# A planner's slot rates, the place of the output weights, and earlier splits in a fused attention and expert-lookup kernel

## The chip, the cores and the metric

The kernel runs on one core of one Trainium2 chip. The metric is device time in microseconds (us), the median of several executions of one program; lower is better.

## The reference

One layer input `x` of 2048 tokens by 512 is normalised, and two branches are added to it.

```python
xn = _layernorm(x, axis=-1)
return x + _A_ref(xn, A_wq, A_wk, A_wv, A_wo) + _B_ref(xn, B_w_q, B_k1, B_k2, B_u, B_v)
```

Branch A is attention with 32 heads of 16 columns that share one key and one value head, with an output projection `wo`. Branch B is a product-key expert lookup: for each token and each of 32 heads, scores against two sets of 64 keys, the two best of each, the two best of the four sums, a softmax over those two, and then, over all chosen experts, `gelu(x . u[expert]) * gate * v[expert]`, with 4096 rows in `u` and in `v`:

```python
act = _gelu(jnp.einsum("nd,nhkd->nhk", xf, ue))
out = jnp.einsum("nhk,nhk,nhkd->nd", g, act, ve)
```

## The kernel before

**Attention sets the beat.** The main loop (L1580 on) runs 256 pairs of key chunks, each for one unit of four heads and 512 tokens. In a pair TensorE forms the scores (`sc`, L448), ScalarE takes four exponentials of 128x1024 (`pt<-sc`, L455), and TensorE forms the weighted values (`pv`, L465). Each pair calls `att_steps` once, which calls `mid` (VectorE and GpSimd work of the expert rows) after the first two exponentials, and `fill` (score and expert matmuls) after the other two. `fill` takes as much work as a linear aim allows (about 3.6 units of planned TensorE time a pair), so every pair carries about the same TensorE work.

**Two ways for the experts.** The tokens fall into four groups of 512. For groups 0 and 1 the chosen rows of `u` and `v` are gathered: 512 slots, each an indirect DMA of 128 rows of 4 KB (`g<-in_uv_dram,idx`, L1180, issued by GpSimd) into one of `NGB = 12` row buffers; a dot with the token rows on VectorE (L1192), four small chain instructions for four slots, and an add of the weighted `v` half (`xa`, L1227), which frees the buffer. For groups 2 and 3 (`dense`, L822 on) one-hot rows are formed on VectorE (`oh`, `obs`, L971 to L974) and multiplied on TensorE (`pg`, L1004) to spread the gates over all 4096 experts, and then 32 blocks of 128 experts are done densely (`pact`, L913; `pout`, L1056). For group 2 each block's rows of `u` and `v` come raw (`rw`) into two buffers with the tag `wqt`, and are split into a high and a low f16 part (`half_split`, L865 to L882: high on ScalarE, L872; low on VectorE, L875), and the parts are also written to DRAM (`ds`); for group 3 the parts are read back, so that the raw rows' buffers are idle then.

**The order of the work.** Score items go group 0, two chunks of group 1, group 2 with its dense part, the rest of group 1, group 3 with its dense part. So there are two dense parts, each led in by some 17 pairs with one-hot rows. A number `dense_on` says where the program is, and a rate table (L1588) says how many slots are planned per pair: 2.5 while indices are being produced ahead, 2.3 for 24 pairs behind a dense part, otherwise 1.75; 0.25 beside one-hot rows (`dense_on` 2), 1.5 at the start of the dense blocks, and 2.5 in the first dense part. From pair 192 on, where the blocks run, all slots that are left are shared out evenly up to pair 252. A slot's gather may be issued when `g_next < a_next + NGB - lent[0]` (L1235): as many slots ahead of the adds as there are buffers, less the lent ones.

**Buffers that are lent.** `load_wo` (L520) brings the output weights `wo` in two tiles. With `lent[0] = 2` they lie in two of the 12 row buffers, and gathers then use 10. `lent[0]` is set at i = 124, 380 and 482 (i counts key chunks, two to a pair) and goes back to 0 when a block of four output tiles is done (L571).

**Query weights.** While group 0 runs, `wp_make` (L628) makes the next chunk's keys-times-weights tiles: four steps of `pw` (L642), then four steps with a transpose (`pwt`, L655), a high part on ScalarE (`wk`, L657) and a low part on VectorE (L658). A sum of squares (`junk`, L613) of a later chunk's weights runs on ScalarE ahead of each of the four high parts. `item` (L679) calls one step of it at k = 0 for the first two of a chunk's four items, at k = 1, and at the end. All of `psc`, `pw`, `pwt`, `pn` and `pact` take turns in three PSUM tiles of tag `x`.

Of the kernel before, what the change touches and what calls it, by code (L numbers as in the profile page):

```python
# [11 lines left out]
F32 = mybir.dt.float32  # L12
# [5 lines left out]
AF = mybir.ActivationFunctionType  # L18
OP = mybir.AluOpType
# [4 lines left out]
P = 128  # L24
S = 2048
D = 512
# [7 lines left out]
NC = 8  # L34
# [26 lines left out]
def tile_kernel(ctx, tc, x, wq, wkv, wo, wqT, kT, uv, ub, vb, out):  # L61
# [453 lines left out]
        ON[pp] = on  # L515

    DONE_A, OUTS = {}, []
    WO, lent = [], [0]

    def load_wo():  # L520
        WO.clear()
        for h in range(2):
            if lent[0]:
                assert g_next[0] - a_next[0] <= NGB - 2
                w = gtile(F32, (P, 2, D), "wo")
            else:
                if h == 0:
                    both = late[0].tile([P, 4, D], F32, name="wo", tag="wd", bufs=2)
                w = both[:, 2 * h:2 * h + 2, :]
            nc.sync.dma_start(w, wo[2 * h * P:2 * (h + 1) * P, :].rearrange("(k p) n -> p k n", p=P))  # L530
            WO.append(w)
# [83 lines left out]
    def wp_factors():  # L615
        c = factored[0]
        factored[0] += 1
        p = xtile("pn")[:, :1]
        for h in range(4):
            nc.tensor.matmul(p, ones_f, squares[:, h:h + 1], start=h == 0, stop=h == 3)  # L620
        x = small.tile([P, 1], F32, name="xw")
        nc.vector.tensor_scalar(x, p, col(K2), None, op0=OP.mult)
        factors(x.bitcast(I32), col(S_W + c), col(I_W + c))

    def wk_tile():
# [2 lines left out]
    def wp_make(c):  # L628

        wt = [big.tile([P, 2, 512], F32, name="wt", tag="da", bufs=2) for _ in range(2)]  # L630
        for h in range(4):
            for n in range(4 * c + h + 1, min(4 * c + h + 5, 4 * NC) if late[0] else 4):
                if ("raw", n // 4, n % 4) not in WC:
                    wp_load(n // 4, n % 4)
            if c == 2 and h > 1:
                wp_square()
            if c > 2 and h == 1:
                wp_factors()
            w = WC.pop(("raw", c, h))
            p = xtile("pw")  # L640
            for s in range(2):
                nc.tensor.matmul(p[s * E:(s + 1) * E, :], kTs[:, s, :], w[:, s, :], start=True, stop=True)  # L642
            nc.scalar.copy(wt[h // 2][:, h % 2, :], p)
            yield 0.9
        WC[c] = []
        if c == 2:
            yield 0.05
            wp_factors()
            yield 0.05
        for k in range(KC):  # L650
            if 1 < c < NC - 1:
                wp_square()
            p = xtile("pwt")
            for h in range(4):
                nc.tensor.transpose(p[:, h * P:(h + 1) * P], wt[h // 2][:, h % 2, k * P:(k + 1) * P], ident)  # L655
            wk = wk_tile()
            nc.scalar.activation(wk[:, 0, :], p, AF.Copy, scale=col(S_W + c))  # L657
            low = lambda p=p, wk=wk: nc.vector.scalar_tensor_tensor(wk[:, 1, :], p, col(S_W + c), wk[:, 0, :],  # L658
                                                                    op0=OP.mult, op1=OP.subtract)
            if c == 1 and late[0] is None:  # L660
                AFTER.append(low)
            else:
                low()
            WC[c].append(wk)
            (store if c > 1 else BULK.append)(lambda k=k, wk=wk: nc.sync.dma_start(d_w[c][:, k], raw(wk[:])))
            yield 0.45
# [12 lines left out]
    def item(n_, ti, make=()):  # L679
        ph, c = SEQ[n_]  # L680
        nph, nc_ = SEQ[n_ + 1] if n_ + 1 < len(SEQ) else (None, None)
        t = TPH * ph + ti
        g, j = divmod(t, GT)
        b, jb = divmod(ti, BT)
        if jb == 0:
            m8 = small.tile([P, BT, 8, 8], F32, name="m8", bufs=1)
            i8 = small.tile([P, BT, 8, 8], U32, name="i8", bufs=1)
            M8[ph, c, b], I8[ph, c, b] = m8, i8
        m8, i8 = M8[ph, c, b], I8[ph, c, b]
        p = xtile("psc")  # L690

        more = nc_ is not None and not (ph >= NSP and c == NC - 1)
        read = more and n_ + 1 >= NC
        n = 0
        for k in range(KC):
            for a, bb in TERMS:
                nc.tensor.matmul(p, XT[k][:, a, j * P:(j + 1) * P], WC[n_][k][:, bb, :],  # L697
                                 start=n == 0, stop=n == 11)
                n += 1
            if read and ti == 0 and k < 2:  # L700
                wp_read(n_ + 1, range(2 * k, 2 * k + 2))
            if k < KC - 1:
                yield 3 * UNIT
            if k == 1 or k == 0 and (n_ == 1 or ti < 2):

                yield from islice(make, 1)
        if more and nph != ph:
            load_xt(nph, j)
        for s in range(8):
            nc.vector.max(m8[:, jb, s, :], p[:, s * E:(s + 1) * E])  # L710
# [111 lines left out]
    def dense(DG, after):  # L822
# [67 lines left out]
        def later_split(b):  # L890
            def go():
                split(b)
                store(lambda: store(lambda: fetch(b + 2)))
            on_act(go)
# [72 lines left out]
        def onehot(q):  # L967
            if q < NQ:
# [5 lines left out]
                nc.vector.tensor_mul(ob, ob, bc(2, tb, NB))  # L974
                OH[q] = oa, ob

        def first_gates():

            for b in range(3):
                fetch_gates(b)  # L980
# [14 lines left out]
        for q in range(NQ):  # L995
# [30 lines left out]

            POST.append((copies, copy if ql % 2 == 0 else lambda: None))

            if q in (NQ - 16, NQ - 12):
                later_split((NQ - 16, NQ - 12).index(q))  # L1030
            if q == NQ - 3:
                on_act(lambda: halves.__setitem__(2, half_split(2, 0)))
            if q == NQ - 3:
                quiet[0] = 3
            if q == NQ - 2:
                dense_on[0] = 3
                on_act(lambda: halves.__setitem__(3, half_split(3, 0)))
                later_split(2)
            if q == NQ - 1:
                later_split(3)  # L1040
            yield 2.0
        held, ready = [], []
        stt = nc.vector.scalar_tensor_tensor
# [28 lines left out]
        for b in range(NB):  # L1072
# [67 lines left out]
            held.append((wd, vs))  # L1140
            if b > 1:
                yield 3 * UNIT
            if b == 3:
                later_split(4)
            if b == 4:
                dense_on[0] = 1
            for _ in range(b - 1 if b in (2, 3) else 0):
# [234 lines left out]
    def att_steps(d, mid, fill):  # L1382
# [48 lines left out]
            last_out_a(3)  # L1431
        if i == STEPS + 2:
            last_out_b()
        if i in (124, 380, STEPS - 30):
            lent[0] = 2
        if 128 <= i < STEPS and i % 128 == (26 if i // 128 == 2 else 10) or i == STEPS - 10:
            load_wo()
        if i == STEPS - 6:
# [134 lines left out]
    with tc.manual_schedule(engines=ENGINES):  # L1573
# [6 lines left out]
        for d in range(half + 24):  # L1580
# [4 lines left out]
            if dense_on[0] == 1:  # L1585
                pos += 2.5 if d < half * 3 // 4 else max(0.0, NSL - pos) / max(half - 3 - d, 1)
            else:
                pos += (2.5 if len(IDX) < NC * TPH else 2.3 if 0 <= d - since < 24 else 1.75, 0, 0.25, 1.5, 0.5)[dense_on[0]]  # L1588

            todo = max(min(int(pos + 0.001), g_next[0]) - d_next[0], 0) if d else 0  # L1590

# [109 lines left out]
```

## Time and profile before

| | |
|---|---|
| Time, median of 3 runs (lowest to highest) | 1825.48 us (1822.67 to 1826.49) |
| Profiled execution: its own time, its span | 1830.28 us, 1828.5 us |
| Busy share of the span | PE 93%, DVE 87%, ACT 73%, POOL 37% |
| Slots (gathers, dots, adds) | 512 each |
| Exponentials `pt<-sc` | 1024, four to a pair |

PE is TensorE, DVE VectorE, ACT ScalarE, POOL GpSimd; SP issues most transfers. In a row of a group, behind the bar, stand the busy time, the mean ns of one, and the idle time of the engine just before such instructions with what ended it.

### The profile page before, as it was taken

To read this page: it belongs to the slowest core of one execution; us is meant where nothing else is said; L and a number is where in the kernel's file an instruction comes from. 1 tells how busy PE (TensorE), PEld (TensorE's weight loads), DVE (VectorE), ACT (ScalarE), POOL (GpSimd) and SP (SyncE) were. 2 spreads that over 40 slices of the span, in tenths; PEclk is the share of its full clock that TensorE was granted. 3 is DMA by queue.
4 is the path that set the end of the run, shared out by engine and by line. 5 is a ranking of instruction groups with operands and counts; after the bars stand their busy time and mean duration, and the time that the engine had idled before them with its cause. 6 is when DMAs were issued, how large, how long until landed. Compare 5 with 4: busy or idle time off the path is not lost.

```text
span 1828.5 us, 35039 instructions
## 1 busy us (share of the span) xinstructions
PE 1708.1 (93%) x11070; PEld 602.5 (33%) x11070; DVE 1592.1 (87%) x6345; ACT 1328.2 (73%) x1785; POOL 684.6 (37%) x923
## 2 busy tenths in 40 slices
PE   7989998999998898999999999999988987899998
PEld 3433332333333332333333333333333322333332
DVE  7748888999998976899998899999989666998995
ACT  6468777867767987888887666666678865677774
POOL 1024444435552102344343455445520124444550
PEclk9999999999999999999999999999999998999999
DMA  7378778998763569999998967966444757999994
GB/s 263 120 255 318 272 241 280 315 325 320 264 218 114 188 218 279 297 336 316 323 336 313 328 237 255 289 201 213 131 147 166 247 183 246 322 315 342 311 300 159
DMA packets 257272, 470.97 MB, mean 258 GB/s; under 512 B 107316, under 2 KB 118596, under 8 KB 257084
## 3 DMA queue, kind: packets, MB, share of 16 engines
q0 software_dynamic: 73728, 268.47, 43.5%
q1 hardware_dynamic: 182940, 199.59, 33.9%
q8 instruction: 87, 1.43, 0.3%
q14 instruction: 101, 0.83, 0.1%
q10 hardware_dynamic: 416, 0.66, 0.1%
HBM read 407.36 MB, written 56.39 MB: 254 GB/s over the span
## 4 chain that ended last, share of the span: by engine, by line
PE 38%; DVE 34%; ACT 7%; DMA 7%; issue 4%; POOL 2%; SPq 0%; another core or an unknown queue 0%; ACTq 0%; DVEq 0%; POOLq 0%
PE pv L465 12%; DVE i L712 7%; PE sc L448 7%; DVE xa L1227 7%; PE pact L913 5%; PE pout L1056 5%; DVE g L1192 5%; DVE m L710 5%; PE psc L697 5%; DMA g<-in_uv_dram,idx 5%; ACT pt L455 4%; DVE oh L971 2%; PE pwo L563 1%; PE pw L642 1%; POOL g L1180 1%
## 5 line engine op out<-in xcount | busy, mean ns | idle before, releaser
L455 ACT ACTIVATE pt<-sc 128x1024 f32<-128x1024 f32 x1024 | 989.1, 1026 | 309.6 <-PE sc L448 254.4
L1180 POOL DMA_INDIRECT g<-in_uv_dram,idx x512 | 541.3, 1057 | 911.7 <-DVE xa L1227 408.6
L465 PE MATMUL pv<-pt,vaug 128*32 128x512 f32 x4096 | 504.3, 611 | 0.0
L448 PE MATMUL sc<-qa,kaug 64*128 64x512 f16 x2048 | 326.8, 385 | 57.9 <-ACT pt L455 50.8
L1227 DVE SCALAR_TENSOR_TENSOR xa<-g,w,xa 128x512 f32<-128x512 f32 x512 | 372.8, 745 | 0.0
L1192 DVE CUSTOM_DVE_ANT_0 g<-g,xa 128x512 f32<-128x512 f32 x512 | 335.0, 682 | 42.6 <-DMA g<-in_uv_dram,idx 41.9
L697 PE MATMUL psc<-wk,xt 128*128 128x512 f16 x1536 | 357.6, 381 | 10.4 <-DVE wk L658 7.5
L448 PEld LDWEIGHTS <-kaug 64*128 64x128 f16 x2048 | 83.6, 94 | 402.2 <-issue 396.9
L697 PEld LDWEIGHTS <-xt 128*128 128x128 f16 x1536 | 141.0, 98 | 208.3 <-issue 59.5
L712 DVE FIND_INDEX8 i<-m,psc 128x8 uint32<-128x64 f32 x1024 | 206.5, 222 | 0.3 <-issue 0.3
L465 PEld LDWEIGHTS pv<-pt,vaug 128*32 128x32 f32 x4096 | 108.3, 110 | 256.9 <-issue 256.9
L913 PE MATMUL pact<-xt,wk 128*128 128x512 f16 x768 | 183.3, 384 | 5.4 <-DVE wk L875 3.9
L1056 PE MATMUL pout<-wk,wd 128*128 128x512 f16 x768 | 176.1, 380 | 1.7 <-DVE gates L1105 1.4
L710 DVE MAX8 m<-psc 128x8 f32<-128x64 f32 x1024 | 146.0, 214 | 10.1 <-PE psc L697 8.8
L913 PEld LDWEIGHTS <-wk 128*128 128x128 f16 x768 | 69.4, 99 | 106.8 <-issue 30.9
L1056 PEld LDWEIGHTS <-wd 128*128 128x128 f16 x768 | 73.2, 98 | 94.9 <-issue 11.0
L971 DVE TENSOR_TENSOR oh<-io,tr 128x2048 f16<-128x2048 f16 x64 | 78.0, 1218 | 9.4 <-ACT tr L939 5.5
L712 DVE MATCH_VALUE_LOAD i<-m,psc 128x8 f32 x1024 | 72.1, 70 | 0.0
L756 POOL CAST fi<-i 128x64 f32<-128x64 uint32 x32 | 8.3, 258 | 148.2 <-DVE i L712 144.5
L1129 DVE SCALAR_TENSOR_TENSOR gy<-gy,pact 128x512 f32<-128x512 f32 x60 | 40.8, 680 | 22.4 <-ACT gy L1128 17.7
L1059 DVE SCALAR_TENSOR_TENSOR da<-pout,cols,da 128x512 f32<-128x512 f32 x72 | 52.9, 744 | 6.1 <-PE pout L1056 4.5
L1208 ACT ACTIVATE gth<-gy 128x4 f32<-128x4 f32 x128 | 26.9, 210 | 41.9 <-DVE gy L1202 33.6
(218 smaller groups left out, 1481.5 us busy)
## 6 DMA issues: line engine op xcount, KB each, us to landing
wk<-dw SPq DMA_DIRECT2D x96, 256.0 KB
wqt<-in_wqT_dram SPq DMA_DIRECT2D x32, 512.0 KB
un<-in_uv_dram SPq DMA_DIRECT2D x16, 1024.0 KB
ds<-wk SPq DMA_DIRECT2D x64, 256.0 KB
gates<-dg SPq DMA_DIRECT2D x64, 256.0 KB
wk<-ds SPq DMA_DIRECT2D x64, 256.0 KB
dg<-gst SPq DMA_DIRECT2D x14, 928.0 KB
dw<-wk SPq DMA_DIRECT2D x32, 256.0 KB
```

The lines of the kernel that those rows point to most:

```text
L448: nc.tensor.matmul(p[:, b, :], kaug[o:o + 64, kc * P:(kc + 1) * P], QA[u][o:o + 64, i, :], start=True, stop=True)
L455: nc.scalar.activation(PT[u, kc, i], p, AF.Exp, scale=SCALE)
L465: nc.tensor.matmul(PV[u][32 * j:32 * j + 32, :], vaug[:, kc, :], pt[:, b, :], start=kc == 0, stop=kc == 15)
L697: nc.tensor.matmul(p, XT[k][:, a, j * P:(j + 1) * P], WC[n_][k][:, bb, :], start=n == 0, stop=n == 11)
L710: nc.vector.max(m8[:, jb, s, :], p[:, s * E:(s + 1) * E])
L712: nc.vector.max_index(i8[:, jb, s, :], m8[:, jb, s, :], p[:, s * E:(s + 1) * E])
L913: nc.tensor.matmul(p, us[:, a, k * P:(k + 1) * P], XT[k][:, c, :], start=n == 0, stop=n == 11)
L971: nc.vector.tensor_tensor(out=oa, in0=num(P), in1=bc(0, tb, P), op=OP.is_equal)
L1056: nc.tensor.matmul(p, wd[0][:, a, j * P:(j + 1) * P], vs[:, c, :], start=n == 0, stop=n == last)
L1180: nc.gpsimd.indirect_dma_start(out=gt, out_offset=None, in_=uv, in_offset=bass.IndirectOffsetOnAxis(ap=IDX[ph, c, ti][:, s:s + 1], axis=0))
L1192: nc.vector.tensor_tensor_reduce(u, u, XN[TPH * ph + ti], scale=1.0, scalar=0.0, op0=OP.mult, op1=OP.add, accum_out=a[:, i:i + 1])
L1227: nc.vector.scalar_tensor_tensor(acc, v, w[:, i:i + 1], acc, op0=OP.mult, op1=OP.add)
```

## The change

The change has five parts:

- The slot rate beside one-hot rows is 0.5 a pair in place of 0.25, and the rate 2.3 behind a dense part holds for 32 pairs in place of 24.
- From i = 380 on no row buffer is lent: `wo` lies in the two raw rows' buffers (tag `wqt`). The first loan, at i = 124, stays.
- In the one-hot stage the splits of blocks 0 to 4 stand at other steps q (of 32). Before: blocks 0 and 1 at 16 and 20, block 2's first half at 29, its rest and block 3's first half at 30, block 3's rest at 31, block 4 in the dense blocks (at b = 3). Now: 14, 17, then 20 and 22 for block 2, 24 and 26 for block 3, 28 and 30 for block 4.
- The four squares that stand beside a chunk's transposes come 0, 2, 1, 1 in place of 1, 1, 1, 1, and only chunk 1's items call a step of `wp_make` at k = 0.
- The factor of a chunk's scale (`xw`, one column) is taken by ScalarE in place of VectorE.

```diff
+            elif ON_ROWS[0]:
+                w = big.tile([P, 2, D], F32, name="wo", tag="wqt", bufs=2)
...
-        nc.vector.tensor_scalar(x, p, col(K2), None, op0=OP.mult)
+        nc.scalar.activation(x, p, AF.Copy, scale=col(K2))
...
-            if 1 < c < NC - 1:
+            for _ in range((0, 2, 1, 1)[k] if 1 < c < NC - 1 else 0):
                 wp_square()
...
-            if k == 1 or k == 0 and (n_ == 1 or ti < 2):
+            if k == 1 or k == 0 and n_ == 1:
...
+        half = lambda b: on_act(lambda: halves.__setitem__(b, half_split(b, 0)))
+        SPLITS = {NQ - 18: lambda: later_split(0), NQ - 15: lambda: later_split(1),
+                  NQ - 12: lambda: half(2), NQ - 10: lambda: later_split(2),
+                  NQ - 8: lambda: half(3), NQ - 6: lambda: later_split(3),
+                  NQ - 4: lambda: half(4), NQ - 2: lambda: later_split(4)}
...
-            if b == 3:
-                later_split(4)
...
-        if i in (124, 380, STEPS - 30):
+        if i == 124:
             lent[0] = 2
+        if i == 380:
+            ON_ROWS[0] = 1
...
-                pos += (2.5 if len(IDX) < NC * TPH else 2.3 if 0 <= d - since < 24 else 1.75, 0, 0.25, 1.5, 0.5)[dense_on[0]]
+                pos += (2.5 if len(IDX) < NC * TPH else 2.3 if 0 <= d - since < 32 else 1.75, 0, 0.5, 1.5, 0.5)[dense_on[0]]
```

VectorE's queue in the first one-hot stage, from the 22nd one-hot step on, before. `oh` and `obs` are one-hot rows, `gst` the copy of spread gates, `ISA g,act` a slot's dot and `ISA act` the read of its sum.

```order
L974 TENSOR_TENSOR obs<-obs,tr 128x512
L1192 ISA g,act<-g,xa 128x512
L1192 ISA act 128x1
L971 TENSOR_TENSOR oh<-io,tr 128x2048
L973 TENSOR_TENSOR obs<-io,tr 128x512
L974 TENSOR_TENSOR obs<-obs,tr 128x512
L1009 COPY gst<-pg 128x32x16
L971 TENSOR_TENSOR oh<-io,tr 128x2048
L973 TENSOR_TENSOR obs<-io,tr 128x512
L974 TENSOR_TENSOR obs<-obs,tr 128x512
L971 TENSOR_TENSOR oh<-io,tr 128x2048
```

Here one dot stands in a stretch of several one-hot steps. The same place now; `gq`, `gy` and `ga` are the chain of four slots, `wk<-rw` the low part of a split.

```order
L976 TENSOR_TENSOR obs<-obs,tr 128x512
L877 SCALAR_TENSOR_TENSOR wk<-rw,cols,wk 128x512
L1192 ISA g,act<-g,xa 128x512
L1192 ISA act 128x1
L1201 SCALAR_TENSOR_TENSOR gq<-act 128x4
L1202 SCALAR_TENSOR_TENSOR gy<-gq,act 128x4
L1203 TENSOR_TENSOR ga<-act,gg 128x4
L973 TENSOR_TENSOR oh<-io,tr 128x2048
L975 TENSOR_TENSOR obs<-io,tr 128x512
L976 TENSOR_TENSOR obs<-obs,tr 128x512
L1017 COPY gst<-pg 128x32x16
```

Between the same one-hot rows VectorE now has a split's low part and, at this point, the chain of the second four slots of the stage: in the stage stand 8 dots and 8 adds where 4 and 4 stood.

ScalarE's queue while a chunk's weights are made, before: `pt` are exponentials, `junk` squares, `wk` high parts.

```order
L455 ACTIVATE pt<-sc 128x1024 x2
L613 ACTIVATE junk,squares<-wqt 128x1024
L657 ACTIVATE wk<-pwt,cols 128x512
L613 ACTIVATE junk,squares<-wqt 128x1024
L657 ACTIVATE wk<-pwt,cols 128x512
L455 ACTIVATE pt<-sc 128x1024 x2
```

And for a chunk now:

```order
L455 ACTIVATE pt<-sc 128x1024 x2
L659 ACTIVATE wk<-pwt,cols 128x512
L615 ACTIVATE junk,squares<-wqt 128x1024 x2
L659 ACTIVATE wk<-pwt,cols 128x512
L455 ACTIVATE pt<-sc 128x1024 x4
```

The first high part now stands ahead of the squares, the second behind two of them; the sums over a chunk are the same.

More of the change, by code (lines that the diff above doesn't have):

```diff
@@ L517, in tile_kernel @@
     DONE_A, OUTS = {}, []
-    WO, lent = [], [0]
+    WO, lent, ON_ROWS = [], [0], [0]
     def load_wo():
@@ L1027, in dense @@
             POST.append((copies, copy if ql % 2 == 0 else lambda: None))
[L1029 to L1032, printed above, removed]
+            if q in SPLITS:
+                SPLITS[q]()
             if q == NQ - 3:
@@ L1036, in dense @@
                 dense_on[0] = 3
[L1037 to L1040, printed above, removed]
             yield 2.0
```

## The prediction

> **What bounds the kernel now.** I read the page first (busy shares, costliest groups), then the busy times by stage, the exponentials by stage (they count the pairs), the groups of single stages, and the timeline where TensorE stood still.
>
> ```profile
> span 1828.5 us, 35039 instructions
> PE 1708.1 (93%) x11070; PEld 602.5 (33%) x11070; DVE 1592.1 (87%) x6345; ACT 1328.2 (73%) x1785; POOL 684.6 (37%) x923
> L1227 DVE SCALAR_TENSOR_TENSOR xa<-g,w,xa 128x512 f32<-128x512 f32 x512 | 372.8, 745 | 0.0
> L1192 DVE CUSTOM_DVE_ANT_0 g<-g,xa 128x512 f32<-128x512 f32 x512 | 335.0, 682 | 42.6 <-DMA g<-in_uv_dram,idx 41.9
> ```
>
> TensorE and VectorE are both near full, so the question is where one of them waits. VectorE waits for gathered rows in all 42 us. The groups of two dense parts, first and last, say where:
>
> ```profile
> L1192 DVE CUSTOM_DVE_ANT_0 g<-g,xa 128x512 f32<-128x512 f32 x110 | 71.4, 682 | 0.0
> ...
> L1192 DVE CUSTOM_DVE_ANT_0 g<-g,xa 128x512 f32<-128x512 f32 x141 | 92.3, 684 | 42.6 <-DMA g<-in_uv_dram,idx 41.9 <-issue 0.5
> ```
>
> The first row is 723.8 to 1024.1 us (44 pairs, 2.5 slots a pair, 12 row buffers): no wait at all. The second is 1464 to 1795.5 (46 pairs, 141 slots, 3.07 a pair, 10 buffers in the first 8 pairs and the last 11): all of the 42 us. What it costs in time is read from the exponentials, four to a pair:
>
> ```profile
> core 0: us, ACT busy (x), PEclk, DMA share, GB/s
> 1464.00:1693.10 229.10, 115.21 (x121) 0.96 0.87 282
> 1693.10:1795.50 102.40, 62.04 (x64) 1.00 0.91 299
> 723.80:1024.10 300.30, 169.31 (x178) 0.99 0.96 317
> 1173.10:1327.40 154.30, 92.92 (x96) 1.00 0.61 199
> ```
>
> The last 16 pairs take 102.4 / 16 = 6.40 us each, and 24 pairs of score items at 1173 take 6.43: this is the beat when TensorE alone binds, since the planner gives each pair the same TensorE work. The 30 pairs from 1464 to 1693.1 take 7.64. At 6.45 they would take 193.5, so some 35 us are lost there.
>
> ```profile
> 1676.92 0.69 DVE L1192 CUSTOM_DVE_ANT_0 g<-g,xa 128x512 f32<-128x512 f32 x1 [1.93 <-DMA g<-in_uv_dram,idx]
> 1681.66 0.72 ACT L1130 ACTIVATE gy<-gy,cols 128x512 f32<-128x512 f32 x1 [1.22 <-DVE gy L1129]
> 1676.30 1.92 PE L465 MATMUL pv<-pt,vaug 128*32 128x512 f32 x16
> 1683.35 0.39 PE L448 MATMUL sc<-qa,kaug 64*128 64x512 f16 x2 [3.18 <-ACT pt L455]
> 1684.80 3.30 PE L465 MATMUL pv<-pt,vaug 128*32 128x512 f32 x16
> ```
>
> This is one such loss: a dot waits 1.93 us for its rows, the dense block's `gy` behind it on VectorE is late, the tanh and the exponentials behind it on ScalarE too, and TensorE stands for 3.18 us; then 16 matmuls that took 1.92 us take 3.30.
>
> ```profile
> 1464.00:1492.40 28.40, 28.04 (x172) 9.75 (x170) 19.35 (x50) 21.03 (x30) 6.38 (x6) 1.00 0.55 169
> 1492.40:1536.00 43.60, 30.02 (x150) 9.62 (x151) 26.52 (x65) 19.58 (x27) 14.01 (x13) 0.86 0.73 225
> 1536.00:1693.10 157.10, 145.88 (x866) 48.00 (x865) 139.18 (x350) 111.58 (x151) 76.31 (x71) 0.97 0.97 318
> ```
>
> (After the length stand PE, PEld, DVE, ACT and POOL busy, the granted clock, DMA share and rate.) Idle time alone is 229.1 - 203.9 = 25 us; the other 10 are slow matmuls, at a granted clock of 0.86 and 0.97. [...]
>
> **The change part by part.**
>
> *Last dense part, -28 us.* By the rate table 17 pairs beside one-hot rows carry 0.25 more, twice (4.25 each), and 8 pairs 2.3 in place of 1.75 (4.4): 12.9 slots are done earlier, which leaves 46 x 3.07 - 12.9 = 128 slots for the 46 pairs, 2.79 a pair, with 12 buffers throughout. The first dense part waited for nothing at 2.5 and 12 buffers, at a DMA share of 0.96. This one lies between: 12 buffers last 4.3 pairs, against 4.8 there and 3.3 (10 buffers) to 3.9 (12) before. At 3.9, in the 22 pairs from 1536 on, 157.1 - 22 x 6.45 = 15 us were lost, part of it while the queue caught up. DMA demand falls by 12.9 x 128 x 4 KB = 6.8 MB. I keep 7 of the 35 us as still lost, half of those 15 (bounds 2 and 17).
>
> *First one-hot stage, +7.*
>
> ```profile
> core 0: us, PE busy (x) PEld busy (x) DVE busy (x) ACT busy (x) POOL busy (x), PEclk, DMA share, GB/s
> 577.30:658.60 81.30, 69.71 (x902) 29.94 (x891) 78.52 (x133) 75.48 (x93) 6.12 (x4) 1.00 0.48 159
> 658.60:702.90 44.30, 44.07 (x258) 14.82 (x261) 27.00 (x63) 35.72 (x47) 10.29 (x10) 1.00 0.83 268
> 1173.10:1327.40 154.30, 152.92 (x947) 51.49 (x945) 151.92 (x1002) 97.15 (x118) 80.00 (x156) 1.00 0.61 199
> 1345.30:1426.90 81.60, 70.06 (x902) 29.65 (x899) 77.70 (x131) 74.54 (x90) 2.15 (x2) 1.00 0.42 141
> ...
> L875 DVE SCALAR_TENSOR_TENSOR wk<-rw,cols,wk 128x512 f16<-128x512 f32 x3 | 2.2, 744 | 0.0
> ```
>
> VectorE binds this stage (78.5 of 81.3). A slot costs it (335.0 + 372.8) / 512 = 1.38 us, 1.4 with its share of the chain. Four more slots (8 for 4 in the order) are 5.6 us. Of the splits' low parts 3 stood here, some 6 will: 3 x 0.74 = 2.2. One us goes into the 2.8 idle. ScalarE takes 3 more high parts, under its 5.8 idle. What the splits leave, 658.6 to 702.9, is full on TensorE (44.1 of 44.3), so nothing is won there.
>
> *Second one-hot stage, +4.6:* four slots, 5.6, less one us of the 3.9 idle; no splits are formed there.
>
> *Pairs 158 to 165, +4:* 4.4 slots are 6.2 us on a VectorE that has 2.4 us to spare in 154.3 (last but one row). The rest stays as lag and is paid at the one-hot rows' lead-in, which waits for the last item's gates. Bounds 0 and 6.
>
> *Weights of the first phase, -1.*
>
> ```profile
> 205.00:281.00 76.00, 70.73 (x426) 23.68 (x418) 66.41 (x342) 57.06 (x84) 32.11 (x42) 0.96 0.77 256
> 281.00:301.00 20.00, 15.31 (x95) 5.89 (x96) 13.80 (x71) 15.05 (x24) 5.35 (x5) 0.91 0.77 248
> 288.03 0.75 DVE L658 SCALAR_TENSOR_TENSOR wk<-pwt,cols,wk 128x512 f16<-128x512 f32 x1 [4.98 <-ACT wk L657]
> 288.84 2.72 PE L697 MATMUL psc<-wk,xt 128*128 128x512 f16 x6 [2.69 <-DVE wk L658]
> ```
>
> Here TensorE stands 10 us in 96, where a high part sits behind squares on ScalarE and an `x` tile is not freed. With two steps of `wp_make` an item, not three, three, two and none, two waits a chunk for the item just finished go, but each item now takes the tile of the one before it, one step later. One high part a chunk comes ahead of the squares, another behind two. I cannot sign this; -8 to +6. The factor's move takes one column from one queue to another, beside exponentials: 0.
>
> *Placing `wo` in idle buffers, 0:* the two transfers stay; only their place changes.
>
> Sum: -28 + 6.8 + 4.6 + 4 - 1 = -13.6, call it -14. The profiled execution took 1830.3 us (1.8 beside its span) and becomes 1816. It lies 0.26% over the median 1825.5, which goes to **1811.5**.
>
> **Rivals.**
>
> *Gathers wait all the same.* From 1536 to 1693.1 the DMA share was 0.97 at 318 GB/s; if the transfers themselves set the wait, two more buffers only lengthen the queue. Then half of the 28 comes, 14, against 14.4 paid: 1825. Against it: 0.96 at 317 GB/s without a wait in the first dense part.
>
> *VectorE becomes the bound (slower).* Its place is the one-hot stages and pairs 158 to 165: nothing of 7.8 + 5.6 + 6.2 = 19.6 us is absorbed. It decides when the last part gives back less than that, as by idle time alone, 25, less 10 still lost: +5, 1830.
>
> *A stall goes that I leave in place.*
>
> ```profile
> 704.85 2.56 ACT L872 ACTIVATE wk<-rw,cols 128x512 f16<-128x512 f32 x4
> 709.32 0.75 DVE L875 SCALAR_TENSOR_TENSOR wk<-rw,cols,wk 128x512 f16<-128x512 f32 x1
> 710.12 4.45 PE L913 MATMUL pact<-xt,wk 128*128 128x512 f16 x10 [3.88 <-DVE wk L875]
> ```
>
> Block 5 waits for its split; with its slow matmuls some 6 us. The earlier splits stop at block 4, and the four high parts of blocks 5 and 6 stand in ScalarE's queue as before, so I expect it again. If it goes, and the first phase gives 6: -25, 1800.
>
> *GpSimd and VectorE hinder each other.*
>
> ```profile
> L1180 POOL DMA_INDIRECT g<-in_uv_dram,idx x4 | 6.1, 1530 | 53.6 <-DVE xa L1227 53.0 <-issue 0.6
> ```
>
> A gather's issue beside one-hot rows took 1.53 us. If VectorE stood still that long, eight more in the two stages would cost 12: -2, 1823.5. [...] The row shows GpSimd slowed, not VectorE.
>
> **How the numbers follow.** 0.2% is 3.65 us, about what a measurement of this kernel can tell from no change. My forecast has 0.60: its bounds added as squares (up 10, 7, 2 and 1; down 5, 7 and 4) make it -23 to -1, 0.57 faster and 0.03 same. The stall goes: 0.10, faster. Gathers still wait: 0.13, mostly same (0.09), 0.03 faster, 0.01 slower. Hindrance: 0.05, same. VectorE binds: 0.12, slower 0.11, same 0.01. Faster 0.70, same 0.18, slower 0.12. The range 1798 to 1824 takes in the forecast's own range, the stall's case and most of the waiting case; the slower case and an edge of the others stay outside.
>
> **What would show it.** Right: dots in the last dense part wait under 10 us for gathers, and its 30 first pairs take 6.5 to 6.7 us each; both one-hot stages are 4 to 8 us longer with VectorE full; the wait before 710 is there again. Wrong: 20 us or more of waits for gathers at the new rate, a one-hot stage longer by over 12 us, or a first phase (124 to 355) that moves by over 8 us either way.

## The result, and the profile after

The changed kernel takes 1812.81 us (median of 5 runs, 1808.76 to 1815.56), the kernel before 1826.49 us beside it (5 runs, 1822.67 to 1828.03): a ratio of 0.9925, 95% interval 0.9908 to 0.9942, or some 13.7 us. The profiled execution took 1814.29 us with a span of 1812.6, 15.9 us less than the span of before. The forecast was 1811.5. The sum came out, but several of its terms did not come about as they were argued, and that is what most of the experiments are on.

The rows of the page of the changed kernel that answer to the first ones of before:

```profile
span 1812.6 us, 35046 instructions
PE 1705.5 (94%) x11070; PEld 601.1 (33%) x11070; DVE 1592.4 (88%) x6337; ACT 1328.8 (73%) x1793; POOL 685.1 (38%) x923
L1227 DVE SCALAR_TENSOR_TENSOR xa<-g,w,xa 128x512 f32<-128x512 f32 x512 | 372.2, 745 | 0.0
L1192 DVE CUSTOM_DVE_ANT_0 g<-g,xa 128x512 f32<-128x512 f32 x512 | 334.3, 682 | 2.6 <-DMA g<-in_uv_dram,idx 2.6
```

The engines do the same work, but the dots' waits for gathered rows fell from 42.6 to 2.6 us. The busy times by stage, first one-hot stage, pairs 158 to 181, second one-hot stage, and then the last dense part in three pieces (us, then PE, PEld, DVE, ACT and POOL busy, granted clock, DMA share, rate):

```profile
572.20:662.90 90.70, 73.65 (x898) 30.07 (x891) 87.54 (x155) 77.47 (x98) 7.55 (x6) 0.94 0.50 171
1176.80:1332.20 155.40, 149.04 (x908) 49.52 (x906) 153.19 (x985) 93.34 (x115) 82.44 (x160) 0.99 0.64 213
1356.30:1444.60 88.30, 74.44 (x904) 30.36 (x896) 83.07 (x147) 74.83 (x92) 10.49 (x8) 0.94 0.55 178
1481.30:1535.30 54.00, 53.89 (x320) 18.38 (x316) 48.02 (x117) 40.57 (x56) 20.99 (x20) 1.00 0.83 263
1535.30:1676.90 141.60, 140.20 (x866) 47.09 (x864) 127.35 (x315) 110.14 (x148) 66.46 (x62) 1.00 0.96 314
1676.90:1779.30 102.40, 102.13 (x632) 34.46 (x630) 93.59 (x234) 78.23 (x104) 41.88 (x39) 1.00 0.86 289
```

In the last dense part TensorE is now full throughout, at a granted clock of 1.00: 30 pairs take 54.0 + 141.6 = 195.6 us, 6.52 each, where they took 229.1. The stages above it became longer. Counted by the exponentials (pair d begins with exponential 4d), the time went like this, in us; columns 4 to 6 are kernels of the experiments below:

| Pairs | before | after | `wo` alone | rates alone | `wo` and first phase |
|---|---|---|---|---|---|
| 5 to 60 (weights of the first phase) | 386.2 | 381.4 | 385.4 | 382.8 | 378.5 |
| 65 to 82 (first one-hot stage) | 81.3 | 90.7 | 81.3 | 88.3 | 81.2 |
| 89 to 91 (block 5's stall) | 20.8 | 21.3 | 21.4 | 20.8 | 20.9 |
| 135 to 158 | 149.0 | 148.0 | 148.5 | 148.0 | 148.4 |
| 158 to 181 | 148.1 | 155.4 | 148.2 | 154.7 | 148.4 |
| 184 to 201 (second one-hot stage) | 81.6 | 88.3 | 83.2 | 86.0 | 81.6 |
| 207 to 215 (last dense part) | 72.0 | 54.0 | 54.1 | 54.0 | 54.0 |
| 215 to 237 | 157.1 | 141.6 | 150.7 | 141.2 | 148.3 |
| 237 to 253 | 102.5 | 102.4 | 102.5 | 102.4 | 102.5 |

The last dense part gives 33.6, the first phase with what lies ahead of pair 65 5.1 (pair 65 begins at 572.2, before at 577.3); the one-hot stages take 9.4 and 6.7, pairs 135 to 181 6.3. That is -33.6 - 5.1 + 9.4 + 6.7 + 6.3 = -16.3, against -15.9 in the spans. One-hot stages at the same slot rate differ by up to 3 us between kernels, and the granted clock goes with it. At the old rate the second one took 81.6 to 81.9 us at a clock of 1.00, 83.2 at 0.98 and 84.8 at 0.96; at the new rate 85.5 to 86.0 at 0.98, and 88.2 and 88.3 at 0.94. The two kernels compared here stand at opposite ends, 1.00 before and 0.94 after, so some 2 us of the 6.7 go with the clock of this execution.

The groups of the first one-hot stage on VectorE, before and after:

```profile
L971 DVE TENSOR_TENSOR oh<-io,tr 128x2048 f16<-128x2048 f16 x31 | 37.7, 1218 | 1.5 <-PE pg L1004 1.5
L1192 DVE CUSTOM_DVE_ANT_0 g<-g,xa 128x512 f32<-128x512 f32 x5 | 3.4, 673 | 0.0
L1227 DVE SCALAR_TENSOR_TENSOR xa<-g,w,xa 128x512 f32<-128x512 f32 x4 | 2.8, 744 | 0.0
```

```profile
L973 DVE TENSOR_TENSOR oh<-io,tr 128x2048 f16<-128x2048 f16 x31 | 37.8, 1218 | 1.1 <-PE pg L1012 1.0
L1192 DVE CUSTOM_DVE_ANT_0 g<-g,xa 128x512 f32<-128x512 f32 x10 | 6.7, 679 | 0.0
L1227 DVE SCALAR_TENSOR_TENSOR xa<-g,w,xa 128x512 f32<-128x512 f32 x8 | 5.7, 745 | 0.0
L877 DVE SCALAR_TENSOR_TENSOR wk<-rw,cols,wk 128x512 f16<-128x512 f32 x7 | 5.2, 746 | 0.0
```

Five dots, four adds and four low parts more (7, where 3 stood) are 3.3 + 2.9 + 3.0 = 9.2 us, and VectorE's busy time rose by 87.5 - 78.5 = 9.0 in a stage that became 9.4 longer: the added instructions were paid in full. This is a long execution of the stage, though: with 11 and with 10 row buffers (below), at the same rate and with the same splits, it took 88.7 and 88.5 us at a granted clock of 0.98, with 8 dots and 8 adds, and VectorE idle for 2.7 and 2.4 us. The one-hot operation itself takes 1218 ns as before. Block 5's stall stands where it stood:

```profile
709.05 2.56 ACT L874 ACTIVATE wk<-rw,cols 128x512 f16<-128x512 f32 x4
713.52 0.75 DVE L877 SCALAR_TENSOR_TENSOR wk<-rw,cols,wk 128x512 f16<-128x512 f32 x1
714.33 4.45 PE L915 MATMUL pact<-xt,wk 128*128 128x512 f16 x10 [3.88 <-DVE wk L877]
```

### The profile page after: what moved, and what is told of

Read it like the earlier page. It is cut to its first block, busy times and chain, and to the rows that moved or that the text cites. A ratio compares the mean times of both kernels' runs of the same rounds, so it can differ in the third digit from the quotient of the medians.

```text
span 1812.6 us, 35046 instructions
## 1 busy us (share of the span) xinstructions
PE 1705.5 (94%) x11070; PEld 601.1 (33%) x11070; DVE 1592.4 (88%) x6337; ACT 1328.8 (73%) x1793; POOL 685.1 (38%) x923
## 4 chain that ended last, share of the span: by engine, by line
PE 58%; DVE 20%; ACT 8%; issue 3%; DMA 3%; POOL 1%; SPq 0%; ACTq 0%; DVEq 0%; another core or an unknown queue 0%; POOLq 0%
PE pv L465 17%; PE sc L448 10%; PE psc L699 10%; PE pout L1058 8%; PE pact L915 7%; ACT pt L455 5%; DVE i L714 4%; DVE xa L1227 3%; DVE m L712 3%; DVE g L1192 3%; PE pwo L565 2%; DVE oh L973 2%; PE pw L644 1%; ACT wk L874 1%; DMA rsb<-dinv 1%
## 5 line engine op out<-in xcount | busy, mean ns | idle before, releaser
L1227 DVE SCALAR_TENSOR_TENSOR xa<-g,w,xa 128x512 f32<-128x512 f32 x512 | 372.2, 745 | 0.0
L973 DVE TENSOR_TENSOR oh<-io,tr 128x2048 f16<-128x2048 f16 x64 | 77.9, 1218 | 10.0 <-PE pg L1012 4.7
L1110 DVE SCALAR_TENSOR_TENSOR gy<-gy,gates 128x512 f32<-128x512 f32 x60 | 41.4, 690 | 22.1 <-ACT gy L1132 17.3
```

The lines of the kernel that those rows point to most:

```text
L973: nc.vector.tensor_tensor(out=oa, in0=num(P), in1=bc(0, tb, P), op=OP.is_equal)
L1227: nc.vector.scalar_tensor_tensor(acc, v, w[:, i:i + 1], acc, op0=OP.mult, op1=OP.add)
```

## The experiments

**The parts one by one.** The first four kernels each have one part of the change on the kernel before (1825.44 us beside them, 1821.87 to 1831.22). The theory (A in each) is the prediction's: waits for gathers in the last dense part come from too few slots of look-ahead, and every other part acts where it stands.

*The place of `wo` alone.*

```diff
+            elif ON_ROWS[0]:
+                w = big.tile([P, 2, D], F32, name="wo", tag="wqt", bufs=2)
...
-        if i in (124, 380, STEPS - 30):
+        if i == 124:
             lent[0] = 2
+        if i == 380:
+            ON_ROWS[0] = 1
```

> The kernel before with the output weights placed in the raw rows' buffers alone; rates, splits and first phase as before. Theory A (how many row buffers lie ahead decides the wait for gathers): the first 8 pairs of the last dense part, which had 10 buffers, go from 72 to about 54 us; the 22 pairs behind them, at 12 buffers and 3.07 slots a pair, keep some 5 of the 15 us they lost; the one-hot stages and pairs 158 to 180 are unchanged. The whole is 25 us faster, 1800. Theory B (the slot rate, and with it the transfers' own rate, decides): the last part stays within 6 us of before, 1820 to 1826.

Measured: 1805.82 us (1802.62 to 1806.52), ratio 0.9875 (0.9854 to 0.9896). The dots of its trace:

```profile
L1194 DVE CUSTOM_DVE_ANT_0 g<-g,xa 128x512 f32<-128x512 f32 x512 | 333.9, 680 | 21.3 <-DMA g<-in_uv_dram,idx 21.3
```

Half of the waits are gone, 24.3 us of the last part's loss come back, and next to nothing is paid for it. Theory A holds for the first 8 pairs (54.1 us); the 22 behind them keep more than its 5 us (150.7, where the changed kernel takes 141.6). This one part is faster than the whole change.

*The rates alone*, 0.5 beside one-hot rows and 32 pairs at 2.3, with buffers lent as before.

```diff
-                pos += (2.5 if len(IDX) < NC * TPH else 2.3 if 0 <= d - since < 24 else 1.75, 0, 0.25, 1.5, 0.5)[dense_on[0]]
+                pos += (2.5 if len(IDX) < NC * TPH else 2.3 if 0 <= d - since < 32 else 1.75, 0, 0.5, 1.5, 0.5)[dense_on[0]]
```

> The kernel before with the two slot rates alone (0.5 beside one-hot rows, 2.3 held for 32 pairs); two row buffers stay lent. Theory A: one-hot stages +6.7 each, pairs 158 to 180 +7; the last part at 2.79 slots and 10 buffers (3.6 pairs of rows ahead) gets back some 15 of 35 us; the whole 5 us slower, 1831. Theory B: the last part gets back 30 or more, the whole 10 us faster, 1816.

Measured: 1811.41 us (1807.62 to 1811.87), ratio 0.9913 (0.9894 to 0.9932). Theory A, by which the rates do little without the buffers, falls. The last part gets back all 34 us, with 9.9 us of waits left, and the stages ahead pay 7.0, 6.6 and 4.4. So rates and place do not add: either removes the pile-up of pairs 207 to 215, and with the rates there is nothing left for the place to win there.

*The earlier splits alone.*

```diff
+            if q in SPLITS:
+                SPLITS[q]()
...
-            if b == 3:
-                later_split(4)
```

> The kernel before with the earlier splits alone. Theory A: VectorE binds the first one-hot stage, so the low parts that move into it cost 2 to 3 us there, and nothing comes back, since TensorE was full behind it and block 5's split waits as before: 1829. Rival: the splits relieve the start of the dense blocks, and the stage 658 to 724 us gets 3 to 6 us shorter: 1823.

Measured: 1827.12 us (1821.62 to 1834.69, 10 runs), ratio 1.0005 (0.9987 to 1.0022): no difference to be told. The first one-hot stage took 83.1 for 81.3, the stall 20.8 as before.

*The first phase's edits alone*: squares, steps of an item, and the factor.

```diff
-            if 1 < c < NC - 1:
+            for _ in range((0, 2, 1, 1)[k] if 1 < c < NC - 1 else 0):
...
-            if k == 1 or k == 0 and (n_ == 1 or ti < 2):
+            if k == 1 or k == 0 and n_ == 1:
```

> The kernel before with the three edits to the first phase alone (two steps of weight making an item, squares 0, 2, 1, 1, the factor on ScalarE). Theory A: pairs 5 to 31 get 4 us shorter as in the changed kernel, all else stays: 1822. Rival: those 4 us are chance of one execution, and the time is that of before, 1826.

Measured: 1824.28 us (1816.83 to 1828.15, 10 runs), ratio 0.9988 (0.9971 to 1.0004). The interval holds both no change and 5 us; pairs 5 to 60 took 380.3 us in the trace, against 386.2.

**Taking parts together.** Three kernels beside one another, and one on look-ahead (the kernel before beside them: 1826.9 us, 1824.73 to 1829.55).

*The change without the earlier splits* (the lines of `SPLITS` left as they were before).

> The changed kernel with the old places of the splits of blocks 0 to 4; everything else as changed. Theory A (every part acts only in the stretch where its instructions stand, and the earlier splits only add three low parts of 0.74 us to a full VectorE in the first one-hot stage): that stage, 90.7 us with all parts, goes to 88 (as with the rates alone, 88.3), the rest stays, 1810 us against 1812.8. Theory B (the earlier splits relieve the dense blocks that follow, so that they pay together with the rates): pairs 82 to 91, 65.8 us, get longer by 3 or more, 1815.

Measured: 1808.63 us (1807.19 to 1811.13), ratio 0.99 (0.9882 to 0.9918). The first one-hot stage took 88.1, the pairs behind it 65.1 as ever. Theory A. The splits' part is 2.6 us here, but at clocks of 0.94 and 0.98; alone it is 1.8 us at 1.00, where the six kernels without splits and at the old rate agree within 0.1 us.

*The same without the new rates*: the place of `wo` and the first phase's edits alone.

```diff
-2.3 if 0 <= d - since < 32 else 1.75, 0, 0.5, 1.5, 0.5)
+2.3 if 0 <= d - since < 24 else 1.75, 0, 0.25, 1.5, 0.5)
```

> The kernel before with the place of wo and the first phase's edits (squares, steps, factor); rates and splits stay old. Theory A (the gains of the two stretches add): 1805.8 with the place alone, less 1.2 to 3, so 1803 to 1804.6, and the last dense part as with the place alone (54 for pairs 207 to 215, 151 for 215 to 237). Theory B (the first phase's gain is only the spread of executions): 1806, no difference from the place alone.

Measured: 1795.3 us (1793.82 to 1802.03), ratio 0.9836 (0.9809 to 0.9862). 8 us better than theory A, most of it because pairs 5 to 60 took 378.5 us, 6.9 less than with the place alone. Beside the last kernel, on the same chip, the new rates cost 1808.63 - 1795.3 = 13.3 us (11.7 by the two ratios). The trace says how: they save 148.3 - 141.2 = 7.1 in pairs 215 to 237, and take 6.9 in the first one-hot stage, 6.2 in pairs 158 to 181 and 6.6 in the second one-hot stage (at a clock of 0.94 for 1.00), together 19.7.

*The slots moved to where VectorE has room.* In the pairs behind each one-hot stage VectorE was busy for 27.0 of 44.3 us and less.

```diff
-1.75, 0, 0.25, 1.5, 0.5)
+1.75, 0, 0.25, 2.25, 0.5)
...
-                    sums = min(sums, 2)
+                    sums = min(sums, 3 if dense_on[0] == 3 and d > 80 else 2)
```

> As the one with the place of wo and the first phase's edits, and the slots that the change takes beside one-hot rows are taken instead in the 7 and 6 pairs behind them, where VectorE was busy for 27 of 44 and 21 of 37 us: the rate there is 2.25 in place of 1.5, and up to 3 adds a pair in place of 2. Theory A (a slot costs time only where VectorE is full): 13 x 0.75, some 9.75 slots leave the last dense part, whose pairs 215 to 237 go from 151 to 144 or less, the 13 pairs take 1 us more at most, both one-hot stages stay at 81 to 83: 1797. Theory B (those pairs carry the first blocks' chains on VectorE, and more dots ahead of them hold TensorE up, or leave no rows ahead for the dense part): those pairs or the ones behind them get 7 us longer, 1804 or more.

Measured: 1796.5 us (1791.72 to 1801.92), ratio 0.9823 (0.9796 to 0.985), no better than the kernel without it. Both theories hold in part: pairs 215 to 237 took 141.1 (148.3), but pairs 89 to 91 grew from 20.9 to 23.7 and pairs 91 to 158 by 3.9, behind the first one-hot stage; the wait of block 5's matmuls itself is 3.95 us for 3.88, and what the rest comes from was not followed. Behind the second one-hot stage nothing got longer.

*Four buffers lent in place of two, with the new rates.*

```diff
-            lent[0] = 2
+            lent[0] = 4 if i == 380 else 2
```

> The kernel before with the new rates alone, and with 4 row buffers lent in place of 2 from i = 380 until the output block is done, so that gathers use 8 there. Theory A (a dot waits when its gather is issued less than some 8 us ahead of it, and that lead is set by the slots between gather and add over the slots a pair, so a lower rate and more buffers stand for each other): at 2.8 slots a pair 8 buffers give a lead as short as 10 did at 3.07, dots wait again 15 us or more in pairs 207 to 215, which go from 54 back to 65 to 80, and the time from 1811.4 to 1820 to 1835. Theory B (what counts is the demand on the transfers that the rate sets, not the buffers): waits stay near 10 us, 1812.

Measured: 1806.2 us (1803.38 to 1809.27), ratio 0.989 (0.9871 to 0.9909), and pairs 207 to 215 took 54.0. This reads as theory B, but the trace shows that the test was none. By the program's count the gathers of slots 380 and 381 come in pair 203, which began at 1446 us. GpSimd in that stretch, with four lent, and with two:

```profile
start us, us, engine line op out<-in xcount [idle before <-releaser]
1409.40 1.15 POOL L1180 DMA_INDIRECT g<-in_uv_dram,idx  x1 [33.01 <-DVE xa L1227]
1413.20 1.88 POOL L1180 DMA_INDIRECT g<-in_uv_dram,idx  x1 [2.66 <-DVE rc L503]
```

```profile
1412.44 1.20 POOL L1180 DMA_INDIRECT g<-in_uv_dram,idx  x1 [30.86 <-DVE xa L1227]
1413.94 0.96 POOL L1180 DMA_INDIRECT g<-in_uv_dram,idx  x1 [0.30 <-issue]
```

The two gathers go at the same place in both. The program's count only sets where a gather stands in the code; GpSimd has its instructions in the same order in both kernels and ran ahead (with four lent, 33 us before pair 203 began); what held the first of the two gathers was an add (33.01 and 30.86 us of idle, `<-DVE xa L1227`), which frees a buffer, and not the count. While the program lends four, slots 380 to 407 go out with nine others between gather and add (one with eight), ten buffers in all, as with two lent from slot 382 on; the count would allow eight. So the look-ahead here was the ten buffers that were really free for it. The kernel is in effect another run of the rates alone.

**The buffers themselves.** So the next two kernels have fewer of them: the changed kernel with 10, and with 11 (beside the kernel before, 1827.68 and 1826.06 us).

```diff
-NGB = 12
+NGB = 10
```

> The changed kernel with 10 row buffers in place of 12 in the whole run (with 4 less that the program lends, gathers were issued as early as with 2 less, since a gather is held on the chip by its buffer and not by the program's count; here the buffers themselves are fewer). Theory A (look-ahead and rate stand for each other: at 2.8 slots a pair ten buffers are 3.6 pairs, between the 3.3 that cascaded into waits and the 3.9 that lost 9 of 157): dots wait 15 to 30 us in the last dense part, half of it is lost, 1820 to 1828. Theory B (the rate alone decides, ten are enough at 2.8 as in pairs 207 to 215 with the rates alone): waits at most 10 us, 1813 to 1816. The first dense part at 2.5 a pair, 4 pairs ahead, stays at 300 us in both.

Measured: 1875.27 us (1870.36 to 1882.09), ratio 1.0282 (1.0235 to 1.0329). Theory A, and far beyond it: two buffers are worth 62 us. In the profiled executions the difference is 57 us, and not all of it lies in the last dense part: pairs 215 to 237 take 28.0 more and pairs 237 to 253 9.6, but pair 65 also begins 11.1 us later, pairs 91 to 135 take 4.6 more, and 253 to 255 6.2. Dots wait 13.3 us for gathers ahead of pair 65 and 8.7 in the first dense part, where they waited for nothing with 12 buffers and where the expectation saw no loss. What makes pairs 253 to 255 longer was not followed. The dots of pairs 215 to 237, and the busy times of that stretch:

```profile
L1192 DVE CUSTOM_DVE_ANT_0 g<-g,xa 128x512 f32<-128x512 f32 x61 | 40.9, 684 | 40.3 <-DMA g<-in_uv_dram,idx 40.1
```

```profile
1494.30:1548.30 54.00, 53.89 (x320) 18.38 (x316) 44.45 (x109) 40.67 (x56) 18.75 (x18) 1.00 0.83 259
1548.30:1717.90 169.60, 147.26 (x866) 48.21 (x864) 129.26 (x322) 111.20 (x149) 66.98 (x62) 0.96 0.85 267
1717.90:1829.90 112.00, 104.52 (x632) 34.97 (x630) 89.98 (x224) 78.50 (x103) 45.98 (x43) 0.98 0.79 257
```

The first eight pairs take no longer than with 12 buffers; there a dot's gather was issued 9.0 us ahead (median), behind them 7.5. The transfers are less busy than with 12 buffers (0.85 against 0.96): it is not their rate that is short. And with 11:

> The changed kernel with 11 row buffers in the whole run. With 12 its dots in pairs 215 to 237 were issued 11.1 us ahead (median) and waited 2.6 us in all, with 10 it was 7.5 us and 40.3 us. Theory A (the lead falls smoothly with the buffers, some 1.8 us a buffer, and waits grow fast below 9 us, as in the kernel before, 8.7 us and 18.2 us): lead 9 to 9.5 us, 8 to 18 us of waits in those pairs, which take 146 to 154 us, and 1818 to 1835 us in all. Theory B (adds free the buffers in fours, so that 11 buffers hold no more than 10, and only a third group of four makes the difference): lead 7.5 to 8 us, 35 us or more of waits, 1865 to 1875.

Measured: 1814.45 us (1809.35 to 1815.65), ratio 0.993 (0.9911 to 0.995). The waits are theory A's, the lead, 8.8 us, a little under it; the total lies 4 us below its range, since these waits cost 4.4 us and those of pairs 237 to 253, 9.3 us, nothing (102.4 us as with 12):

```profile
L1192 DVE CUSTOM_DVE_ANT_0 g<-g,xa 128x512 f32<-128x512 f32 x61 | 40.3, 682 | 14.0 <-DMA g<-in_uv_dram,idx 13.7
```

Here are all kernels in pairs 215 to 237. The lead is the time from a gather's issue on GpSimd to its dot on VectorE, both in slot order, and its median is given; a dot counts where it begins.

| Kernel | Buffers | Dots there | Lead, us | Waits, us | Length, us |
|---|---|---|---|---|---|
| 10 buffers, new rates | 10 | 61 | 7.5 | 40.3 | 169.6 |
| earlier splits alone | 12 | 69 | 8.6 | 17.8 | 156.3 |
| before | 12 | 69 | 8.7 | 18.2 | 157.1 |
| `wo` and first phase | 12 | 68 | 8.7 | 11.9 | 148.3 |
| `wo` and squares (below) | 12 | 68 | 8.7 | 11.7 | 149.3 |
| first phase alone | 12 | 69 | 8.8 | 20.9 | 160.4 |
| 11 buffers, new rates | 11 | 60 | 8.8 | 14.0 | 146.0 |
| `wo` alone | 12 | 68 | 8.9 | 15.1 | 150.7 |
| best (below) | 12 | 65 | 9.1 | 5.3 | 141.3 |
| rates alone | 12 | 61 | 10.0 | 2.9 | 141.2 |
| slots moved | 12 | 61 | 10.3 | 0.8 | 141.1 |
| four lent, new rates | 12 | 61 | 10.5 | 3.8 | 141.2 |
| without the splits | 12 | 59 | 10.8 | 1.8 | 141.2 |
| after | 12 | 59 | 11.1 | 2.6 | 141.6 |

Lead goes up with buffers and down with slots a pair. From 10 us on the waits are under 4 us, at 7.5 they are 40; close to 9 us the median does not order the kernels (11.7 to 20.9 us of waits at leads of 8.6 to 8.9). In the eight traces that have landings for this stretch, the median from a gather's issue to its landing is 6.5 to 7.5 us, so that a median lead of 7.5 us leaves next to nothing over. The lead goes the same way in pairs 207 to 215, where either part removes the pile-up: it was 8.4 us there before, with 22.2 us of waits, 9.2 with the rates alone (6.8 us of waits), 9.6 with the place alone (2.5) and 15.2 with both (none). Some 5 us of waits in 22 pairs cost nothing (the best version: 5.3 us of waits, and 141.3 us long).

**The first phase.** The place of `wo` with the squares 0, 2, 1, 1 alone:

```diff
-            if 1 < c < NC - 1:
+            for _ in range((0, 2, 1, 1)[k] if 1 < c < NC - 1 else 0):
```

> The kernel before with the place of wo (1805.8) and the squares 0, 2, 1, 1; steps of an item as before. Theory A (the gain of the first phase, pairs 5 to 60 from 385 to 380, comes from the first high part of a chunk, which no longer stands behind a square): pairs 5 to 60 take 379 to 382, 1800 to 1802. Theory B (it comes from two steps an item in place of three): 384 to 387, 1804 to 1807.

Measured: 1801.62 us (1798.45 to 1806.23), ratio 0.9877 (0.984 to 0.9915). Pairs 5 to 60 took 379.7 us: theory A. Before, and with the squares moved:

```profile
152.10:538.30 386.20, 369.19 (x2266) 126.22 (x2261) 361.19 (x2107) 294.18 (x415) 181.75 (x287) 0.98 0.85 286
```

```profile
148.70:528.40 379.70, 364.26 (x2254) 125.68 (x2246) 360.81 (x2107) 294.65 (x414) 181.51 (x287) 1.00 0.86 290
```

Of the 6.5 us only 1.6 are idle time of TensorE (17.0 to 15.4); the other 4.9 are its busy time, at a granted clock of 1.00 for 0.98. In the traces of the kernels before and after, the clock falls to half 14 and 13 times for 3.41 or 6.83 us, and once for less at the end of each. The first such stretch in the kernel before, with the wait ahead of it:

```profile
218.87 0.63 PE L655 MATMUL pwt<-ident,wt 128*128 128x128 f32 x4 [2.65 <-DVE i L712]
219.90:223.30 3.40, 3.40 (x18) 0.73 (x20) 3.04 (x8) 2.26 (x3) 0.14 (x1) 0.50 0.89 308
```

Pairs 5 to 60 have four of them before (from 219.9, 237.0, 288.2 and 376.9 us) and one with the squares moved (from 230.3). Three stretches fewer, at half the clock, are 3 x 3.41 / 2 = 5.1 us, which accounts for the 4.9. The longest single waits ahead of these five were 2.65, 1.10, 2.69, 2.06 and 1.10 us. The number of stretches is partly chance: the five kernels with the old squares have two to four and take 382.9 to 386.9 us, the seven with the new ones and 12 buffers (all but this one with the item's steps and the factor too) one or two and 378.5 to 381.4. With half the time of its stretches taken off, the five are at 379.3 to 380.3 and the seven at 376.3 to 378.7, so some 2 us come by the waits and the rest by how often the clock fell. The ratio alone does not tell this kernel from the one with `wo` alone (0.9875).

**The best version.** From `wo` and the first phase: the higher rate behind the second one-hot stage alone, the earlier splits, and block 5's split asked for a block sooner, which the earlier split of block 4 allows.

```diff
-1.75, 0, 0.25, 1.5, 0.5)
+1.75, 0, 0.25, 2.25 if d > 128 else 1.5, 0.5)
...
-                    sums = min(sums, 2)
+                    sums = min(sums, 3 if dense_on[0] == 3 and d > 128 else 2)
...
+                        if b == 2 and DG == NSP:
+                            later_split(5)
+                        elif b == 3 and DG > NSP:
+                            later_split(5)
...
-            if b % 2 and b > 1:
+            if b % 2 and b > 3:
                 later_split(b + 2)
```

> The kernel with the place of wo and the first phase's edits (1795.3), and three things more: the rate 2.25 and up to 3 adds behind the second one-hot stage alone; the earlier splits; and block 5's split asked for in block 2 in place of block 3. Theory A (each acts in its stretch): pairs 215 to 237 from 148 to 142; pairs 89 to 91 from 20.9 to 13 to 15, since block 5's low part no longer stands in VectorE's queue behind a block's gy; pairs 65 to 82 from 81.2 to 83 for the splits' low parts; 1785 to 1788. Theory B (block 5 waits for its raw rows, which the first blocks' transfers hold up, and the stall only moves): pairs 89 to 93 keep their length, and the splits' cost remains, 1791 to 1794.

Measured: 1787.96 us (1783.16 to 1790.66), ratio 0.9799 (0.9764 to 0.9834), the fastest of all kernels here, 37 (by the ratio) to 40 us (by the medians) below the kernel before. Theory A holds in each of its figures. The stall is gone, and with it its slow matmuls; the first matmuls of the two blocks in pairs 89 to 91, and then the busy times of pairs 89 to 91 and 215 to 237:

```profile
701.36 2.12 PE L915 MATMUL pact<-xt,wk 128*128 128x512 f16 x9
708.93 2.12 PE L915 MATMUL pact<-xt,wk 128*128 128x512 f16 x9
```

```profile
699.00:712.50 13.50, 11.59 (x68) 3.96 (x61) 11.80 (x28) 12.28 (x18) 4.09 (x4) 1.00 0.98 278
1504.60:1645.90 141.30, 140.21 (x866) 47.13 (x864) 132.54 (x335) 110.06 (x149) 71.22 (x66) 1.00 1.01 329
```

No wait stands before these matmuls, and the two pairs take 13.4 us for 20.9. Pairs 65 to 89 pay 3.2 of it (82.9 + 45.9, against 81.2 + 44.4). The last row has the DMA engines at a share of 1.01, and TensorE still full.

## Why the prediction was right, and where its steps failed

- **Last dense part, -28: measured -33.6.** The mechanism was right and the 7 us that I kept as still lost were not lost. They were set by slots per buffer between two rows; by the lead, 11.1 us, the stage was clear of the waits. The 10 us that I put down to slow matmuls are right: the first 30 pairs had the clock at half for 20.5 us, which costs 10.2, and with the waits gone it was 1.00 in all 30. Which waits bring such a stretch about was not found: in the first phase they stand behind waits of 1.10 to 2.69 us.
- **Two buffers and fewer slots as one cause: wrong as a sum.** The prediction put both into the one term and gave the place of `wo` 0 by itself. The place alone gives 24.3 of the 33.6, the rates alone 34.0; together they give no more than the rates. "12 buffers throughout" was the free half of the term, and I let the rates carry it.
- **First one-hot stage, +6.8: measured +9.4.** The slots and low parts were counted nearly right (9.2 us by their rows, with one low part and one dot more than I had), but the one us that I took off for VectorE's idle 2.8 was not there: idle time was 3.2 after. With 11 and 10 buffers the stage became 7.4 and 7.2 longer, with idle times of 2.7 and 2.4. The other 2 us here go with the clock, 0.94 for 1.00, for which the sum had no term.
- **Second one-hot stage, +4.6: measured +6.7.** The size was right but for the clock. VectorE's busy time rose by 83.1 - 77.7 = 5.4 and its idle time from 3.9 to 5.2, at a clock of 0.94. The four kernels that ran this stage at the new rate and 0.98 took 3.9 to 4.4 us more than before, with VectorE idle for 2.7 to 3.2: there about one us of the idle time was used, as I had it.
- **Pairs 158 to 165, +4: measured +6.3** over pairs 135 to 181 (5.5 and 5.6 with the rates alone and without the splits). The 2.4 us of idle VectorE that were to take part of it did not: in pairs 158 to 181 they are 2.2 in every kernel at the new rates, as before, and those pairs grew by 6.4 to 7.3. The three terms together are 22.4 us in this execution, where 15.4 were forecast, and some 17 in the kernels with the clock at 0.98.
- **Weights of the first phase, -1 (-8 to +6): about -5.** I could not sign it; the squares' order gives it, some 2 us by waits and the rest by how often the granted clock fell, which differs between executions. The factor's move was not tried by itself.
- **Block 5's stall stays: right**, and it went when block 5's split was asked for a block sooner, in the best version.
- **The rivals.** *VectorE becomes the bound* had its mechanism right in two of its three places, where nothing was absorbed, and it was outweighed only because the last part gave back all. *Gathers wait all the same* falls: with a DMA share of 1.01 and 65 dots the last part ran at TensorE's pace, and with 10 buffers and a share of 0.85 it did not. *GpSimd and VectorE hinder each other* does not show: the one-hot operation took 1218 ns before and after, with six gathers beside it in place of four. Only a gather's issue took longer in the first one-hot stage, 1.53 us before and 1.26 after in the mean, where the mean of all 512 is 1.06.

So the three terms that came dearer (by 7.0 us) and the two that gave more (by 5.6 and some 4) cancelled but for some 3 us of the profiled execution. That the time came out so close to the forecast is in part luck. The change as a whole is a gain, but its rates are a loss on top of its buffers: 13.3 us of what the place of `wo` and the squares give is handed back.

What stays open: how much the earlier splits cost beside the new rate (at a clock of 0.98 the first one-hot stage takes 88.5 and 88.7 us with them and 88.1 and 88.3 without), and whether the rate beside one-hot rows or the longer hold of 2.3 is the dearer, which were only run together. The rates and the place of `wo` were not run with nothing else, and what halves the clock behind one short wait and not behind another was not found.

## What to carry to other kernels

Two remedies for one wait did not add here (24.3 and 34.0 us alone, 33.6 together): cost each alone first, and take the one that is free, here an idle buffer, before one that moves work onto a full engine. Work that was moved into stages where VectorE was busy for 95 to 98% was paid in full there, or nearly so (in the first one-hot stage 9.0 us of work made it 9.4 longer), so look for the stretch where that engine has room, and then for who is queued behind. Measure look-ahead as the time from issue to use in the trace, beside the time that a transfer takes to land; here that told kernels with long waits from those with next to none, when the DMA shares did not, and left only those close to the edge unordered. And before a difference of 2 us in a stage is put down to its instructions, look at the granted clock of both executions.

## What the runs showed of the hardware that was not expected

- A count in the program did not hold a gather back. With 4 buffers lent by the count GpSimd issued slots 380 and 381 at 1409.4 and 1413.2 us, as with 2 (1412.4 and 1413.9), the first behind 33.0 and 30.9 us of idle that an add ended.
- The price of a buffer was a cliff: with 12, 11 and 10 the kernel took 1812.81, 1814.45 and 1875.27 us, with 2.6, 14.0 and 40.3 us of waits for gathers in pairs 215 to 237, and with 10 more of them elsewhere (13.3 us ahead of pair 65, where 12 buffers have none).
- Waits on TensorE cost more than themselves: with 10 buffers 7.1 of the 28.0 us lost in pairs 215 to 237 were slower matmuls (147.3 us for the same 866 recorded matmuls that took 140.2 with 12; the clock was at half for 13.7 us there, which costs 6.8), and in the first phase some 5 of 6.5 us.
- The clock fell to half for 3.41 or 6.83 us but at the end of a kernel (27 times before and after), and it did so behind waits as short as 1.1 us (four stretches before and one with the squares moved in pairs 5 to 60, behind longest waits of 1.10 to 2.69 us).
